# The 128 half rows of w_down: loaded ahead of wq into a buffer of their own

## The chip, the cores and the metric

The kernel runs on one core of one Trainium2 chip. The metric is the device time of one execution in microseconds (us). Before the change it is 202.81 us, the median of three runs (202.72 to 202.81).

The core has the engines TensorE (PE; its weight loads are listed as PEld), VectorE (DVE), ScalarE (ACT), GpSimd (POOL) and SyncE (SP). SP issues nearly all loads here; 16 DMA engines carry them.

## What is computed

One token goes through one decoder layer: attention over a cache of 4,096 positions with 32 heads of 128, then a gated feed-forward part. All tensors are bf16.

```python
x = A_x                                             # 1 x 640
q = layernorm(x) @ wq                               # 640 x 4096, 32 heads of 128
p = softmax(q . k_cache / sqrt(128))                # 32 heads, 4096 positions
h = x + (p . v_cache) @ wo                          # 4096 x 640
g = layernorm(h) @ w_gate                           # 640 x 1728
u = layernorm(h) @ w_up                             # 640 x 1728
out = h + (gelu(g) * u) @ w_down                    # 1728 x 640
```

The tensors that have to be read are large beside the arithmetic: k_cache and v_cache have 33.6 MB each, wq and wo 5.2 MB each, w_gate, w_up and w_down 2.2 MB each.

## The kernel before

**Heads and slots.** The 32 heads are handled in 8 groups of 4. One load brings K or V of one group (4,096 KB, 128 partitions x 32 KB) into one of three slots (`slots`, L114). The order of loads (L191) is K0, V0, K1, V1 and so on to V5, then K6, K7, V6, V7; load n goes to slot n modulo 3, and waits for the last reader of load n - 3 (`issue`, L201 to L209).

**A group's work.** For K: four products of a quarter slot with the query on DVE (L295, `prod`), each summed over part of the head dimension by eight matmuls with the identity on PE (L305 and L29) and by a reduction on DVE (L312). Then the maximum (L317 to L320), the exponential on ACT (L323) and its spreading over four columns on DVE (L326). For V: 32 matmuls (L341 and L29), a masking product and a reduction on DVE (L353 and L363). `matmul_again` (L27, so L29 in the profile) issues a matmul that keeps the weights of the one before.

**The order on each engine.** Each engine has a list of operations, filled by the Python code from top to bottom, and runs it in that order. `P.op` and `P.dma` append to such a list; `_run` (L91) puts a wait ahead of an operation for each event that it depends on. `P.emit({"sync": 2})` (L581) puts the first two operations of SP's list ahead of the barrier that ends the program's preamble; all others stand behind it. As the list of SP stands, these two are the load of wq (L190) and that of K0.

**SP's list.** The load of wq into the arena, the 16 loads of K and V, two loads of wo into the arena (L454 and L455, 2,560 KB each, after the query projection has read wq there), and then the weights of the feed-forward part. These reuse two slots: w_gate and w_up go to the slot that held V6 (`sl[0]`), w_down to the slot that held K7 (`sl[1]`). `free[0]` is the last V6 matmul and `free[1]` the last K7 product (L457).

**w_down.** Its 1,728 rows are split: rows 0 to 1535 as three blocks of 4 x 128 rows (`wd_d`, loaded in four pieces of 640, 640, 480 and 160 KB), rows 1536 to 1663 as one block (column ranges of 64 and 96 KB at the end of the list), and the last 64 rows as 128 half rows of 320 columns (L464; 640 B in each of the 128 partitions, 80 KB), two halves of a row side by side in neighbouring partitions. The half rows went to place 13 of the buffer `wd_sb`, so their load waited for `free[1]`, and it stood first behind wo.

**The last steps.** After the last group, the attention output is multiplied with wo (L399), the residual and the second LayerNorm follow (L480 to L500), then the gate products (L508, `ga`), the up products, gelu on DVE and ACT, and the down products (L558). The down products run block by block: blocks 0 to 3, the half rows (`down([13])`, five matmuls, with the activations doubled and masked in `hm2`), blocks 4 to 7, 8 to 10, 11, and 12 in four column ranges, each followed by a copy to `out_row` (L575 and L577). The output is then stored (L578).

Of the kernel before, what the change touches and what calls it, by code (L numbers as in the profile page):

```python
# [6 lines left out]
BF16 = mybir.dt.bfloat16  # L7
# [4 lines left out]
D = 640  # L12
# [98 lines left out]
def bass_sequential_preLN__gqa_block_cached__glu_gated_geglu__decode_kernel(nc, A_x, A_k_cache, A_v_cache, A_wq, A_wo, B_x, B_w_gate, B_w_up, B_w_down, out):  # L111
    sb = lambda name, shape, dt: nc.alloc_sbuf_tensor(name, shape, dt)
# [41 lines left out]
    sel2 = sb("sel2", [64, 64, 2], BF16)  # L154
    par_t = sb("par_t", [128, 2, 64], BF16)
    par = sb("par", [128, 2], FP32)
    one_bf = sb("one_bf", [1, 1], BF16)
    ones_f = sb("ones_f", [128, 128], FP32)
    mean_f = sb("mean_f", [128, 128], FP32)
# [13 lines left out]
    ps_d = bank[4][:, 264:456]  # L173
# [7 lines left out]
    P = Prog(nc)  # L181
# [5 lines left out]

    A(lambda e: e.preload_act_table_set("natural_log_exp_and_others"))
    d_x = P.dma("scalar", x_row[:, :], A_x[0, :, :])
    d_wq = [P.dma("sync", arena[:, :], A_wq[:, :].rearrange("(p c) n -> p (c n)", c=5))]  # L190
    order = [(kind, G) for G in range(NG - 2) for kind in "KV"] + [(kind, G) for kind in "KV" for G in (NG - 2, NG - 1)]  # L191
    pos = {t: n for n, t in enumerate(order)}
# [251 lines left out]
    for kind, G in order:  # L444
# [3 lines left out]
        if G != NG - 2:  # L448
# [8 lines left out]
    free = [consumed[len(order) - NSLOT + i] for i in (1, 0)]  # L457
    wg_sb = sl[0][:, 0:5 * DF].rearrange("p (c n) -> p c n", c=5)
    wu_sb = sl[0][:, 5 * DF:10 * DF].rearrange("p (c n) -> p c n", c=5)
    wd_sb = sl[1][:, 0:14 * D].rearrange("p (m n) -> p m n", m=14)  # L460
    wu_v = B_w_up[:, :].rearrange("(p c) n -> p c n", c=5)
    wd_v = B_w_down[0:1536, :].rearrange("(a p r) n -> p a r n", a=3, r=4)
    wd_d = wd_sb[:, 0:12, :].rearrange("p (a r) n -> p a r n", a=3)
    d_wd = [P.dma("sync", wd_sb[:, 13, 0:320], B_w_down[1664:1728, :].rearrange("f (s n) -> (f s) n", s=2), free[1])]  # L464
    d_wg = P.dma("sync", wg_sb, B_w_gate[:, :].rearrange("(p c) n -> p c n", c=5), free[0])
    d_wu = [P.dma("sync", wu_sb[:, 0:3, :], wu_v[:, 0:3, :]),
            P.dma("sync", wu_sb[:, 3:5, :], wu_v[:, 3:5, :])]
    d_wd += [P.dma("sync", wd_d[:, a, lo:hi, :], wd_v[:, a, lo:hi, :])
             for a, lo, hi in ((0, 0, 4), (1, 0, 4), (2, 0, 3), (2, 3, 4))]
    d_wl = [P.dma("sync", wd_sb[:, 12, a:b], B_w_down[1536:1664, a:b]) for a, b in (CUT[0:3:2], CUT[2:5:2])]  # L470

# [8 lines left out]
    hi = [V(lambda e: e.tensor_copy(A_hi[0:97, 0:320], bank[0][0:97, 0:320]), pr),  # L480
          A(lambda e: e.copy(A_hi[0:97, 320:640], bank[1][0:97, 0:320]), pr)]
    lo = [V(lambda e, t=t: e.tensor_sub(A_lo[0:97, 320 * t:320 * t + 320], bank[t][0:97, 0:320], A_hi[0:97, 320 * t:320 * t + 320]),
            hi[t]) for t in range(2)]
# [63 lines left out]
    def down(ms, qs=range(4)):  # L547
        def fn(e):
            for m in ms:
                for q in qs:  # L550
                    lo, hi = CUT[q], CUT[q + 1]
                    if m < 13:
                        parts = [(hm[:, m:m + 1], lo, hi, 0)]
                    else:
                        parts = [(hm2[:, s:s + 1], max(lo, 320 * s), min(hi, 320 * s + 320), 320 * s) for s in range(2)]
                    for w, a, b, base in parts:
                        if a < b:
                            i = e.matmul(ps_d[32 * q:32 * q + 1, a - lo:b - lo], w, wd_sb[:, m, a - base:b - base],  # L558
                                         start=False, stop=(m == 12), skip_group_check=(m == 13))
            return i  # L560
        return fn
# [48 lines left out]
```

## Time and profile before

| | |
|---|---|
| median of the runs | 202.81 us |
| the profiled execution's own time | 202.6 us |
| its span, first to last instruction | 201.3 us |
| DVE busy | 136.4 us (68%) |
| PE busy | 114.6 us (57%) |
| bytes read, mean rate | 84.23 MB, 418 GB/s |
| SP's loads (queue q1), share of 16 engines | 97.9% |
| wq, issue to landing | 15.3 us |
| half rows of w_down, issue to landing | 13.7 us |
| mean granted clock of PE | 0.828 |

The profile is of one execution. Its times count from the span's start. An engine is busy while it executes; issuing a load is not counted as busy. A packet of a DMA is here one row of one partition; a packet record has its start, duration and size. Landing is the moment at which the last of the 16 engines reports its share of a load. The granted clock is the part of TensorE's full speed that the throttle allowed; here it changes between 1.0 and 0.5. A wait is put down to what came last. A merged line of the timeline ("x20") covers several instructions.

### The profile page before, as it was taken

How to read it: one execution, taken by the hardware profiler on the slowest of the kernel's cores; microseconds unless marked ns; L12 is line 12 of the kernel's file. 1: busy time of each engine (PE TensorE's matmuls, PEld its weight loads, DVE VectorE, ACT ScalarE, POOL GpSimd, SP SyncE). 2: the span in 40 equal slices, each digit the busy share in tenths (PEclk: the TensorE clock that was granted, in tenths of full speed). 3: DMA queues.
4: the chain of work that ended last, by engine and by line, in shares of the span. 5: the costliest groups of instructions: out<-in, count | busy, mean ns of one | idle time of the engine just before them, and what ended most of it. 6: DMA issues, size and time to landing. Idle time of an engine off the chain costs nothing.

```text
span 201.3 us, 1448 instructions
## 1 busy us (share of the span) xinstructions
PE 114.6 (57%) x785; PEld 17.8 (9%) x381; DVE 136.4 (68%) x168; ACT 8.9 (4%) x27; POOL 4.7 (2%) x14
## 2 busy tenths in 40 slices
PE   0108059537736962777169618762774099386485
PEld 0101000000001000100010001000100001021332
DVE  1300188637995999399757985996799978862531
ACT  2100000000000000000000000000000000000111
POOL 7100000000000000000000000000000000000000
PEclk9999757996995899699757975998899859967575
DMA  9999999999999999999999999999999999999992
GB/s 350 423 392 462 449 417 417 417 443 462 433 430 417 412 423 436 456 449 423 417 417 420 449 449 443 423 417 423 423 462 430 443 423 400 431 415 430 414 407 104
DMA packets 4185, 84.31 MB, mean 419 GB/s; under 512 B 466, under 2 KB 980, under 8 KB 1492
## 3 DMA queue, kind: packets, MB, share of 16 engines
q1 hardware_dynamic: 4178, 84.23, 97.9%
q8 instruction: 4, 0.07, 0.1%
q14 instruction: 1, 0.01, 0.0%
q10 hardware_dynamic: 2, 0.00, 0.0%
HBM read 84.23 MB, written 0.00 MB: 418 GB/s over the span
## 4 chain that ended last, share of the span: by engine, by line
DMA 54%; DVE 28%; PE 15%; SPq 1%; issue 1%; ACT 0%
DMA slot<-in_A_k_cache_dram 41%; DVE prod L295 18%; DMA slot<-in_B_w_down_dram 13%; PE bank L29 10%; DVE sc L312 5%; DVE po_r L363 3%; PE bank L341 2%; PE bank L305 2%; SPq L60 1%; DVE p_bd L326 1%; PE bank L558 1%; DVE mx L317 1%; DVE mxd L319 0%; DVE mxd L318 0%; DVE nb L320 0%
## 5 line engine op out<-in xcount | busy, mean ns | idle before, releaser
L295 DVE TENSOR_TENSOR prod<-slot,qb 128x4096 bf16<-128x4096 bf16 x32 | 72.5, 2286 | 20.8 <-DMA slot<-in_A_k_cache_dram 20.8
L29 PE MATMUL bank<-prod,id_b 128*128 128x512 bf16 x224 | 61.2, 419 | 0.0
L305 PE MATMUL bank<-prod,id_b 128*128 128x512 bf16 x32 | 14.1, 440 | 36.2 <-DVE prod L295 36.1
L341 PE MATMUL bank<-slot,p_bd 128*32 128x512 bf16 x128 | 17.7, 542 | 27.4 <-DVE p_bd L326 27.4
L312 DVE TENSOR_REDUCE sc<-bank 128x32 f32<-128x512 f32 x32 | 22.0, 688 | 9.6 <-PE bank L29 9.5
L29 PE MATMUL bank<-slot,p_bd 128*32 128x512 bf16 x128 | 18.0, 550 | 0.0
L305 PEld LDWEIGHTS bank<-prod,id_b 128*128 128x128 bf16 x32 | 3.3, 102 | 89.8 <-DVE prod L295 89.6
L363 DVE TENSOR_REDUCE po_r<-po_m 128x128 f32<-128x1024 f32 x6 | 11.2, 1865 | 0.0
L353 DVE TENSOR_TENSOR po_m<-bank,m 128x1024 f32<-128x1024 f32 x8 | 9.7, 1218 | 1.6 <-PE bank L29 1.6
L323 ACT ACTIVATE p_t<-sc,nb 128x128 bf16<-128x128 f32 x8 | 3.2, 401 | 150.6 <-DVE nb L320 150.6
L341 PEld LDWEIGHTS bank<-slot,p_bd 128*32 128x32 bf16 x128 | 4.3, 122 | 54.2 <-DVE p_bd L326 40.2
L285 DVE CAST qb<-bank 128x512 bf16<-128x512 f32 x1 | 0.7, 692 | 9.9 <-PE bank L29 9.9
L280 PE MATMUL bank<-arena,xlnB 128*32 128x512 bf16 x20 | 3.3, 627 | 7.1 <-DMA arena<-in_A_wq_dram 7.1
L326 DVE TENSOR_TENSOR p_bd<-p_t,hs 128x512 bf16<-128x512 bf16 x8 | 5.5, 682 | 1.1 <-ACT p_t L323 1.1
L369 PE MATMUL bank<-po_r,hs 128*16 128x129 f32 x16 | 4.3, 367 | 0.8 <-DVE po_r L361 0.8
L399 PE MATMUL bank<-arena,aP 128*1 128x320 bf16 x32 | 4.0, 440 | 0.9 <-DMA arena<-in_A_wo_dram 0.9
L508 PE MATMUL bank<-slot,hlnT 128*1 128x512 bf16 (+1 forms) x40 | 3.5, 450 | 1.5 <-DVE hlnT L497 1.5
L252 PE MATMUL bank<-one_bf,x_row 1*128 1x1 bf16 x5 | 0.4, 177 | 6.9 <-DMA x_row<-in_A_x_dram 6.9
L29 PE MATMUL bank<-arena,aP 128*1 128x320 bf16 x32 | 3.9, 436 | 0.0
L29 PE MATMUL bank<-arena,xlnB 128*32 128x512 bf16 x20 | 3.2, 607 | 0.0
L558 PE MATMUL bank<-slot,hm 128*1 128x128 bf16 (+2 forms) x57 | 2.6, 301 | 0.4 <-DMA slot<-in_B_w_down_dram 0.4
L369 PEld LDWEIGHTS bank<-po_r,hs 128*16 128x16 f32 x16 | 2.0, 130 | 7.4 <-issue 5.8
(89 smaller groups left out, 45.8 us busy)
## 6 DMA issues: line engine op xcount, KB each, us to landing
slot<-in_A_k_cache_dram SPq DMA_DIRECT2D x8, 4096.0 KB, 19.1
slot<-in_A_v_cache_dram SPq DMA_DIRECT2D x8, 4096.0 KB, 18.8
arena<-in_A_wq_dram SPq DMA_DIRECT2D x1, 5120.0 KB, 15.3
arena<-in_A_wo_dram SPq DMA_DIRECT2D x2, 2560.0 KB, 27.6
slot<-in_B_w_gate_dram SPq DMA_DIRECT2D x1, 2160.0 KB, 18.5
slot<-in_B_w_up_dram SPq DMA_DIRECT2D x1, 1296.0 KB, 21.1
slot<-in_B_w_down_dram SPq DMA_DIRECT2D x2, 640.0 KB, 24.4
slot<-in_B_w_up_dram SPq DMA_DIRECT2D x1, 864.0 KB, 22.7
```

Of the source, the lines that this page charges most:

```text
L29: return e.add_instruction(mybir.InstMatmult(name=nc.get_next_instruction_name(), engine=e.engine, start_tensor_calc=start, stop_tensor_ca ...
L295: m = V(lambda e: e.tensor_tensor(out=prod[:, s % 4, :, :], in0=kt[:, 32 * u:32 * u + 32, :], in1=qb[:, G, :].unsqueeze(1).to_broadcast([1 ...
L305: i = e.matmul(*args, start=True, stop=False)
L312: reds[s] = V(lambda e: e.reduce_sum(sc[:, (s // 4) % 2, s % 4, :], ps_f[s % 2][:, :].rearrange("p (g d) -> p g d", d=16), axis=AX.X), fol ...
L326: pbs[G] = V(lambda e: e.tensor_tensor(out=p_bd[:, G % 2, :, :], in0=p_t[:, G % 2, :].unsqueeze(2).to_broadcast([128, 128, 4]), in1=hs[:, ...
L341: return e.matmul(*args, start=(c < 4), stop=(c >= 12))
L353: mks[G] = V(lambda e: e.tensor_tensor(out=po_m[:, :, :], in0=po[:, :].rearrange("p (b d) -> p b d", b=8), in1=m8[:, :].unsqueeze(2).to_br ...
L363: evs[G] = V(lambda e: e.reduce_sum(po_r[:, G % 4, 0:DH], po_m[:, :, :].rearrange("p b d -> p d b"), axis=AX.X), mks[G], hds.get(G - 4))
L369: return e.matmul(ps_a[0:16, 132 * (G // 4):132 * (G // 4) + DH + 1], hs[:, 12 - 4 * g:28 - 4 * g], po_r[:, G % 4, :], start=(g == 0), sto ...
L399: r = e.matmul(*args, start=start, stop=stop)
L508: i = e.matmul(po[32 * a:32 * a + 1, 512 * k:512 * k + n], hlnT[:, c:c + 1], w[:, c, 512 * a:512 * a + n], start=(c == 0), stop=(c == 4))
L558: i = e.matmul(ps_d[32 * q:32 * q + 1, a - lo:b - lo], w, wd_sb[:, m, a - base:b - base], start=False, stop=(m == 12), skip_group_check=(m ...
```

## The change

A buffer `wh_sb` of 128 x 320 elements is added. The half rows are loaded into it by the first load of SP's list, with no wait. The four pieces of the three w_down blocks name `free[1]` as what they wait for, which the half rows' load had waited for ahead of them. The down products with the half rows read `wh_sb`. As the number of operations ahead of the barrier stays 2, the load of K0 is now behind it.

```diff
@@ buffers
+    wh_sb = sb("wh_sb", [128, D // 2], BF16)
@@ start of SP's list
+    d_wh = P.dma("sync", wh_sb[:, :], B_w_down[1664:1728, :].rearrange("f (s n) -> (f s) n", s=2))
     d_wq = [P.dma("sync", arena[:, :], A_wq[:, :].rearrange("(p c) n -> p (c n)", c=5))]
@@ behind wo
-    d_wd = [P.dma("sync", wd_sb[:, 13, 0:320], B_w_down[1664:1728, :].rearrange("f (s n) -> (f s) n", s=2), free[1])]
     d_wg = P.dma("sync", wg_sb, B_w_gate[:, :].rearrange("(p c) n -> p c n", c=5), free[0])
     d_wu = [P.dma("sync", wu_sb[:, 0:3, :], wu_v[:, 0:3, :]),
             P.dma("sync", wu_sb[:, 3:5, :], wu_v[:, 3:5, :])]
-    d_wd += [P.dma("sync", wd_d[:, a, lo:hi, :], wd_v[:, a, lo:hi, :])
+    d_wd = [d_wh] + [P.dma("sync", wd_d[:, a, lo:hi, :], wd_v[:, a, lo:hi, :], free[1])
              for a, lo, hi in ((0, 0, 4), (1, 0, 4), (2, 0, 3), (2, 3, 4))]
@@ down products
-    i = e.matmul(ps_d[...], w, wd_sb[:, m, a - base:b - base],
+    i = e.matmul(ps_d[...], w, (wd_sb[:, m, a:b] if m < 13 else wh_sb[:, a - base:b - base]),
```

More of the change, by code (lines that the diff above doesn't have):

```diff
@@ L557, in fn @@
                         if a < b:
-                            i = e.matmul(ps_d[32 * q:32 * q + 1, a - lo:b - lo], w, wd_sb[:, m, a - base:b - base],
+                            i = e.matmul(ps_d[32 * q:32 * q + 1, a - lo:b - lo], w, (wd_sb[:, m, a:b] if m < 13 else wh_sb[:, a - base:b - base]),
                                          start=False, stop=(m == 12), skip_group_check=(m == 13))
```

## The prediction

> **What bounds the kernel now.** I read the page first (engine shares, the row of 40 slices, the chain that ended last), then the windows at both ends of the span, SP's own timeline, the chain in order of time, and the packet records of the trace.
>
> ```profile
> span 201.3 us, 1448 instructions
> ...
> DMA  9999999999999999999999999999999999999992
> ...
> DMA 54%; DVE 28%; PE 15%; SPq 1%; issue 1%; ACT 0%
> ```
>
> The reader is to see that the 16 DMA engines are busy in every slice but the last. The chain's 28% DVE and 15% PE are steps beside that stream, passed through because a load was issued when a slot came free; they cost nothing while older loads fill the queues. So the time is: start of the stream + packet time of 84.23 MB + what follows the last landing. A change that moves 80 KB within the stream can act only on the start, the end, or the order of landings.
>
> The start, first by windows (columns: stretch, length, the engines' busy us and counts, granted clock, DMA share, GB/s):
>
> ```profile
> 0.00:1.00 1.00, 0.00 (x0) 0.00 (x0) 0.00 (x0) 0.00 (x0) 0.20 (x4) 1.00 0.00 0
> 1.00:2.00 1.00, 0.00 (x0) 0.00 (x0) 0.38 (x5) 0.74 (x1) 0.74 (x1) 1.00 2.18 655
> ```
>
> A packet is counted where it starts. 655 GB/s over 1 us is 16 packets of 40,960 B, one on each engine: the first row of wq. They occupy 2.18 us each on average. The packet records give 1.51 us for the later rows of wq, so each engine first waited some 0.67 us for data, after about 1.0 us in which nothing ran. Then SP:
>
> ```profile
> 0.00 0.39 SPq L60 DMA_DIRECT2D arena<-in_A_wq_dram  x1
> 0.44 0.42 SPq L60 DMA_DIRECT2D slot<-in_A_k_cache_dram  x1
> 1.26 0.33 SPq L60 DMA_DIRECT2D slot<-in_A_v_cache_dram  x1
> ...
> 152.75 0.91 SPq L60 DMA_DIRECT2D arena<-in_A_wo_dram  x2
> 170.10 0.33 SPq L60 DMA_DIRECT2D slot<-in_B_w_down_dram  x1
> 170.48 0.43 SPq L60 DMA_DIRECT2D slot<-in_B_w_gate_dram  x1
> ```
>
> The second load is issued 0.44 us after the first; the third stands behind the barrier that ends the program's preamble (1.26). The load at 170.10 is the one that moves. And the end, by the chain in order of time:
>
> ```profile
> 172.85 25.67 DMA slot<-in_B_w_down_dram
> 198.52 0.04 issue
> 198.56 1.20 PE bank L558 x17
> 199.76 0.03 issue
> 199.79 0.35 DVE out_row L575
> ```
>
> The 480 KB part of w_down (rows 8 to 10 of the third block) lands at 198.52; the last down products, a copy and the output follow.
>
> **The change part by part.** The order of instructions in the changed program has the same instructions on PE, DVE, ACT and POOL; on SP, one load moves from behind wo to the head. Three things follow.
>
> (1) *At its old place it goes.* The packet records show 128 packets of 640 B with 4.10 us in sum: 4.10 / 16 = 0.256 us on each engine, without a gap, plus 0.009 for the completion. Landing bears it out: issue at 170.10 + 13.7 us (its row of DMA issues, 80 KB) = 183.8, against 183.6 for the second half of wo before it (issue at 153.2, 30.4 us, the longest of the arena's loads). Bounds 0.20 and 0.27; I take **-0.26**. Its 0.33 us of issue on SP also go, at no gain: the loads behind it, issued from 170.48 on, land 18 us and more later, so they stand in a queue.
>
> (2) *At the head it comes in.* The load is issued first, wq 0.44 later. Lower end: wq's data flow only the 0.26 us later that the small packets occupy, when wq's descriptors arrive while the small rows still wait for their first data (0.67 of wait is longer than 0.44 of issue). Upper end by issue: wq's first packet starts 0.44 later and waits as long as now, so everything is 0.44 later and the small rows lie inside that. A far end, that the two waits add up, is a rival below (0.67 + 0.26 = 0.93). A gain at the head has no mechanism except that of the fourth case. I take the middle of the two near ends, **+0.35**, as both rest on a row of their own and the wait covers one of them only in part.
>
> In sentences of their own: the Trainium skill ("DMA: Bandwidth & Descriptors", section "Bandwidth", Measured) speaks against such a load: it gives 0.95 us for 64 KB and says that transfers under 64 KB are dominated by descriptors; those are loads from the other kind of queue, GpSimd's. The trace differs where the load lies in a full queue (0.26 us for 80 KB). Where it stands alone at the head no run shows it; with 0.95 there, an estimate from that page, the sum would be +0.69 and the time 203.3 by the profile, 203.5 by the median.
>
> (3) *The order changes.* K0, now third, moves behind the barrier: 0.44 to 1.26. Cover: wq's 5 MB keep the engines until about 15 (landing 15.3), so 13 us are left; without it K0 would be 0.8 late. V0 and K1 slide by one place, under the same cover. The wait for the slot's last reader (K7's product, DVE, 170.1) moves from this load to the first 640 KB of w_down; w_gate and w_up, 4,320 KB, now wait only for the PE's V6 products (about 168.9 in the timeline), and can be issued 1.6 us earlier. Behind the waiting instruction stand only the rest of w_down's loads and the output; nobody waits for their issue, since the queue then holds both halves of wo until 183.6. So no gain and no loss. The buffer of 640 B per partition is new; the down products with the half rows read it in place of the slot, five matmuls as before.
>
> What is before the old place lands 0.35 later, what is behind it 0.35 - 0.26 = **+0.09** later. That matters once: a compute chain starts with wo's second half.
>
> ```profile
> 183.75 0.43 PE L399 MATMUL bank<-arena,aP 128*1 128x320 bf16 x4 [0.91 <-DMA arena<-in_A_wo_dram]
> ...
> 196.77 1.44 PE L558 MATMUL bank<-slot,hm 128*1 128x128 bf16 x37
> ...
> 198.56 1.15 PE L558 MATMUL bank<-slot,hm 128*1 128x128 bf16 x20 [0.35 <-DMA slot<-in_B_w_down_dram]
> ```
>
> PE waits for wo's landing; from there LayerNorm, gate, up and the first 37 down products follow almost without a load ending last, and the last 20 wait 0.35 us for w_down. The chain is put back by 0.26 against the landing that ends its wait: 0.35 - 0.26 = 0.09 us of slack is left. It still does not set the end.
>
> **Sum**: -0.26 + 0.35 = +0.09, say +0.1 us. On the profiled execution (202.6 us, span 201.3 and 1.3 around it) 202.7. That execution lies 0.2 under the median of the three runs (202.81), so for the median: **202.9 us**. What a measurement of this kernel can tell from no change is about 0.2%, 0.4 us.
>
> **The rivals.**
> - *Slower: the head waits twice.* Place: the engines' start. wq's first rows begin their 0.67 us wait only after the small load is through, so the stream starts 0.93 later and gets 0.26 back: +0.67, 203.3 by the profile, **203.5** for the median. For it: the first packets show a wait that no later packet has, and nothing in the trace shows two such starts overlap. Against it: everywhere else packets follow without gap, so the next descriptors are taken while the last are under way. It counts as slower when wq's first data come over 0.67 us later than now (0.67 - 0.26 = 0.41).
> - *Slower: PE becomes the bound.* The 0.09 us of slack is used up if PE is granted less clock after the gate. In the windows 194 to 197 the granted clock is 1.00, and the 20 up matmuls take 1.25 us; at 0.50, the gate's first 17 take 1.87, that is 2.2 for 20. Then +0.95 - 0.09 + 0.09, about **203.8**. Against it: the three runs agree within 0.09 us, so the grant does not fall differently by chance.
> - *A little faster: a late engine catches up.* The first packets of 15 engines end between 3.22 and 3.68 (packet records), of one at 4.39, and this engine's 16th count ends the 480 KB part at 198.52, the next at 198.35. If the small rows take up its late start, up to 0.17 goes on top of the lower end (0.00): **202.6**; with the other engines' spread (198.22) 202.5.
> - *The change doesn't do what it says: the load is hidden anyway.* As the stream is full, to carry 80 KB earlier saves nothing but position; this is the forecast's core, not another time.
>
> **How the numbers follow.** Forecast (0.00 to +0.18, the sums with both near ends): 0.62, all within 0.2%. Head waits twice: 0.20, of which 0.01 stays within 0.2%. PE bound: 0.06, slower. Late engine: 0.12, of which 0.05 for a gain of 0.4 us and more, if the other engines' spread goes too. Faster 0.05, within 0.2% 0.62 + 0.07 + 0.01 = 0.70, slower 0.25. The range reaches from 202.5 (late engine) to 203.5 (head waits twice); the PE case and the rest outside it hold about 0.15. The forecast's own range is 202.8 to 203.0.
>
> **What would show it.** In the changed profile, the windows at the start should have small packets from about 1.0 us and wq's landing (first q matmul at 15.45 now) 0.26 to 0.44 later; by 0.9 and more if the head waits twice. The idle time of DVE ahead of K0's first product should end that much later than 25.03. The DMA row should stay at 9 until the last slice. wo's second half should land as much later as wq; the last large w_down part between 198.5 and 198.7. PE's wait ahead of the last 20 products should shrink from 0.35 to about 0.1. If wq lands late by more than 0.67, step 2 is wrong; if that wait is gone and the end later than w_down's landing asks for, step 3; if the end does not follow w_down's landing, the reading of the bound.

## The result

The changed kernel takes 203.05 us (median of 17 runs, 202.88 to 203.8), the kernel before, beside it, 202.73 (17 runs, 202.59 to 203.06). The ratio is 1.0018, 95% interval 1.001 to 1.0025: 0.18% or about 0.36 us slower (0.32 us by the medians), clear of noise. The bound of 0.2% lies inside the interval. The profiled execution takes 202.89 us against 202.6.

The page of the changed kernel, its row of slices and its chain by engine:

```profile
span 201.6 us, 1448 instructions
...
DMA  8999999999999999999999999999999999999993
...
DMA 53%; DVE 28%; PE 16%; issue 1%; SPq 0%; ACT 0%
```

The reader is to see that the stream still has no gap, and that the two slices which differ are the first (8 for 9) and the last (3 for 2): it starts later and ends later. SP's timeline and the windows of the start, changed kernel:

```profile
0.00 0.40 SPq L60 DMA_DIRECT2D wh_sb<-in_B_w_down_dram  x1
0.46 0.41 SPq L60 DMA_DIRECT2D arena<-in_A_wq_dram  x1
1.28 0.33 SPq L60 DMA_DIRECT2D slot<-in_A_k_cache_dram  x1
```

```profile
0.00:1.00 1.00, 0.00 (x0) 0.00 (x0) 0.00 (x0) 0.00 (x0) 0.20 (x4) 1.00 0.00 0
1.00:1.50 0.50, 0.00 (x0) 0.00 (x0) 0.15 (x2) 0.23 (x1) 0.23 (x1) 1.00 0.63 164
1.50:2.50 1.00, 0.00 (x0) 0.00 (x0) 0.23 (x4) 1.00 (x1) 0.93 (x2) 1.00 2.33 655
```

164 GB/s over 0.5 us is 82 KB: the small packets all start in this half microsecond, and hold the engines for 0.31 us each (0.63 of 0.5). The 16 first packets of wq (655 GB/s over 1 us) start only behind 1.5. Before, 13 of them started in that half microsecond:

```profile
1.00:1.50 0.50, 0.00 (x0) 0.00 (x0) 0.17 (x2) 0.24 (x1) 0.24 (x1) 1.00 3.59 1065
```

The end, by the chain in order of time and by the timeline of the changed kernel:

```profile
171.49 27.31 DMA slot<-in_B_w_down_dram
198.79 0.04 issue
198.84 0.94 PE bank L559 x16
```

```profile
184.25 0.31 PE L401 MATMUL bank<-arena,aP 128*1 128x320 bf16 x4 [1.17 <-DMA arena<-in_A_wo_dram]
...
193.57 2.16 PE L509 MATMUL bank<-slot,hlnT 128*1 128x512 bf16 x20
...
197.31 0.50 PE L559 MATMUL bank<-slot,hm 128*1 128x128 bf16 x16
...
197.68 0.54 PE L559 MATMUL bank<-slot,hm 128*1 128x128 bf16 x16
...
198.84 1.16 PE L559 MATMUL bank<-slot,hm 128*1 128x128 bf16 x20 [0.61 <-DMA slot<-in_B_w_down_dram]
```

The 480 KB part of w_down lands at 198.79, 0.27 after the time before, and the output follows by as much: the execution is 0.29 longer. That part is not the last one waited for. By the trace's records the products behind it wait for each of the three pieces that are left, and the last weight load starts 0.04 us after the landing of the last 96 KB, before (199.35) as after (199.62). The landings between (records of the trace, the middle of the 16 engines' counts, before and after) say where it comes from:

| landing | before | after | later by |
|---|---|---|---|
| wq | 14.31 | 14.93 | 0.62 |
| wo, second half | 182.07 | 182.67 | 0.60 |
| w_gate | 187.40 | 187.80 | 0.40 |
| w_down, 480 KB | 197.05 | 197.44 | 0.39 |

By wq's landing 0.6 us are lost; they stay lost through 168 us of full stream, and 0.2 come back where the half rows used to lie. The last of the 16 counts, for which the products wait, moves by 0.75 at wq (15.31 to 16.06), 0.51 at wo, 0.29 at w_gate and 0.27 at the end; which engine is last is not the same one throughout.

### The profile page after: what moved, and what is told of

Same layout as the page of the kernel before. It is cut to its first block, busy times and chain, and to the rows that moved or that the text cites. A ratio compares the mean times of both kernels' runs of the same rounds, so it can differ in the third digit from the quotient of the medians.

```text
span 201.6 us, 1448 instructions
## 1 busy us (share of the span) xinstructions
PE 113.6 (56%) x785; PEld 17.3 (9%) x381; DVE 136.2 (68%) x168; ACT 8.9 (4%) x27; POOL 4.7 (2%) x14
## 4 chain that ended last, share of the span: by engine, by line
DMA 53%; DVE 28%; PE 16%; issue 1%; SPq 0%; ACT 0%
DMA slot<-in_A_k_cache_dram 39%; DVE prod L297 18%; DMA slot<-in_B_w_down_dram 14%; PE bank L29 11%; DVE sc L314 5%; PE bank L343 3%; DVE po_r L365 3%; PE bank L307 2%; DVE p_bd L328 1%; DVE mx L319 1%; PE bank L559 0%; DVE mxd L321 0%; DVE mxd L320 0%; SPq L60 0%; DVE nb L322 0%
## 5 line engine op out<-in xcount | busy, mean ns | idle before, releaser
L343 PE MATMUL bank<-slot,p_bd 128*32 128x512 bf16 x128 | 18.3, 561 | 27.3 <-DVE p_bd L328 27.3
L29 PE MATMUL bank<-slot,p_bd 128*32 128x512 bf16 x128 | 18.3, 561 | 0.0
L509 PE MATMUL bank<-slot,hlnT 128*1 128x512 bf16 (+1 forms) x40 | 4.5, 544 | 1.5 <-DVE hlnT L498 1.5
L371 PE MATMUL bank<-po_r,hs 128*16 128x129 f32 x16 | 3.8, 328 | 1.5 <-DVE po_r L363 1.5
L401 PE MATMUL bank<-arena,aP 128*1 128x320 bf16 x32 | 2.5, 301 | 1.2 <-DMA arena<-in_A_wo_dram 1.2
L29 PE MATMUL bank<-arena,aP 128*1 128x320 bf16 x32 | 2.6, 317 | 0.0
L319 DVE TENSOR_REDUCE mx<-sc 128x1 f32<-128x128 f32 x8 | 2.3, 286 | 0.3
```

The source lines that it names most:

```text
L29: return e.add_instruction(mybir.InstMatmult(name=nc.get_next_instruction_name(), engine=e.engine, start_tensor_calc=start, stop_tensor_ca ...
L319: m = V(lambda e: e.reduce_max(mx[:, G:G + 1], sc[:, G % 2, :, :].rearrange("p u g -> p (u g)"), axis=AX.X), reds[4 * G + 3])
L343: return e.matmul(*args, start=(c < 4), stop=(c >= 12))
L371: return e.matmul(ps_a[0:16, 132 * (G // 4):132 * (G // 4) + DH + 1], hs[:, 12 - 4 * g:28 - 4 * g], po_r[:, G % 4, :], start=(g == 0), sto ...
L509: i = e.matmul(po[32 * a:32 * a + 1, 512 * k:512 * k + n], hlnT[:, c:c + 1], w[:, c, 512 * a:512 * a + n], start=(c == 0), stop=(c == 4))
```

## The experiments

Two theories of the loss at the head. The *issue theory*: wq starts later by the distance of two issues on SP, whatever the first load carries, as long as that is through in this time. The *sum theory*: the first load's transfer and a new first wait add up. Each ratio is against the kernel before on the same chip.

**The price of the head, by size.** One more load ahead of wq, everything else as before.

```diff
+    ex_sb = sb("ex_sb", [128, 320], BF16)              # 32 elements for 8 KB, 1,920 for 480 KB (there rows 0 to 383)
+    d_ex = P.dma("sync", ex_sb[:, :], B_w_down[1664:1728, :].rearrange("f (s n) -> (f s) n", s=2))
     d_wq = [...]
```

With 8 KB: 

> The kernel before, with one more load ahead of wq: the first 64 B of each of the 128 half rows (8 KB) into a buffer that nobody reads; the half rows stay at their old place. Issue theory: wq starts later by the distance of two issues on SP (0.46 us in the changed kernel's profile), whatever the size of the first load as long as it is through in that time: +0.5 us against before, wq lands about 0.5 later. Sum theory: wq starts later by the transfer of what is ahead of it and then has its first wait anew, about 0.3: with next to no transfer +0.3 us. If the head costs nothing by itself: 0.0.

With 80 KB: 

> The kernel before, with a second copy of the half rows (80 KB) loaded ahead of wq into a buffer that nobody reads. This is the price of the head alone, without the gain at the old place. Issue theory: the same as with 8 KB, +0.5 us. Sum theory: 0.26 more than with 8 KB, +0.55 us. Both: the changed kernel's +0.3 comes back as this price less about 0.23.

With 480 KB: 

> The kernel before, with 480 KB (rows of 3,840 B, 1.22 us on each engine) loaded ahead of wq into a buffer that nobody reads. Issue theory: wq's issue lies inside the transfer, so the price is the transfer alone, +1.2 us. Sum theory: transfer and a new first wait, +1.5 us.

| ahead of wq | median, before | ratio, interval | wq's first packets: mean start, mean time | wq lands (middle count) |
|---|---|---|---|---|
| nothing (before) | | | 1.28, 2.18 | 14.31 |
| 8 KB | 203.13, 202.72 | 1.0024, 1.0016 to 1.0033 | 1.70, 2.29 | 14.94 |
| 80 KB | 203.20, 202.72 | 1.0027, 1.0017 to 1.0038 | 1.66, 2.37 | 14.92 |
| 480 KB | 203.74, 202.72 | 1.0063, 1.004 to 1.0085 | 2.81, 1.56 | 15.28 |

8 KB cost +0.41 us and 80 KB +0.48; a tenth of the bytes has the same price, and wq lands at the same time. The sum theory wanted 0.25 us between them and falls: the intervals of the two times alone would leave room for it, wq's landings, 14.94 and 14.92, do not. 480 KB cost 1.02 by the medians, below the issue theory's 1.2 and far below the sum theory's 1.5. That interval is wide (0.8 to 1.7 us; one of six runs took 205.3), but the trace agrees: wq lands 0.97 later, w_down's 480 KB part 1.05 (198.52 to 199.57). Behind a transfer longer than SP's next issue, wq's first packets take 1.56 us, hardly more than the 1.51 of all later ones, so their wait passes under the transfer. (The 480 KB rows have a wait of their own: 1.52 us on each engine by the records, where eight packets of 0.149 make 1.19.)

One figure shows why the issue counts. Take the mean start of wq's first packets plus what they take beyond 1.51, and count it from wq's issue: 1.95 us before, 2.04 behind 8 KB (wq issued at 0.44), 2.07 behind 80 KB (0.45), 2.06 in the changed kernel (0.46). wq's data flow about 2 us after wq's issue, with or without a small load ahead; only the 480 KB, which keep the engines until 2.8, make it 2.42. So the price of a small load is the distance of the issues and 0.1 us more. Why the data take 2 us no run shows.

**The same load elsewhere.**

```diff
 half_second:     d_wq = [...]
                 +d_wh = P.dma("sync", wh_sb[:, :], ...)          # behind wq, ahead of K0
 half_act:       +d_wh = P.dma("scalar", wh_sb[:, :], ...)        # ACT's first operation
                 -P.emit({"sync": 2})
                 +P.emit({"sync": 2, "scalar": 1})
 half_old_place: +d_wh = P.dma("sync", wh_sb[:, :], ...)          # behind wo, no wait
```

> The changed kernel with its first two loads exchanged: wq, then the half rows, then K0. Both theories of the head: wq is first again, so the load lies in a full stream as it did behind wo; 0.0 us against before, within 0.1, and wq lands at about 15.3 as before. If instead the new buffer or the moved wait cost the 0.3 us, it stays at +0.3.

Measured 202.76 against 202.72, ratio 1.0001 (0.9993 to 1.001). With the same buffer, the same moved wait and K0 still behind the barrier, the loss is gone as soon as wq is first. wq lands at 14.38, the half rows 0.24 behind it.

> The changed kernel with the half rows' load issued from ACT's queue ahead of the barrier, beside SP's issue of wq instead of ahead of it. Issue theory: SP issues wq at 0.0 again; if the small rows pass in the first wait of the engines, -0.2 us against before, if wq's descriptors wait for theirs, between 0.0 and +0.3. Sum theory: small rows ahead of wq cost as at the head, +0.3; behind wq 0.0.

Measured 202.74 against 202.75, ratio 1.0003 (0.9994 to 1.0012): the 0.0 of the list. ACT issues at 0.12, but the first small packet starts at 3.10, behind the first packet of wq on its engine, and by 8 us only 53 of the 128 have started: they go in among wq's packets. The idle time before the first data is not used.

> The changed kernel with the half rows' load back behind wo, still into the buffer of its own and still without a wait: the buffer and the moved wait alone. Both theories of the head: 0.0 us against before, within 0.1. If the buffer or the moved wait cost something, up to +0.3.

Measured 202.93 against 202.75, ratio 1.0009 (1.0000 to 1.0018). This is inconclusive by itself; the run with the load in second place has the same buffer and wait and costs nothing, so I don't put a price on either.

**The gain at the old place, and K0.**

> The changed kernel without the load of the half rows: their buffer is set to zero by POOL, so the last 64 rows of w_down are left out of the result. This is the gain at the old place alone: -0.26 us against before by the packet records (bounds 0.20 and 0.27), under either theory of the head.

Measured 202.47 against 202.75, ratio 0.9992 (0.9983 to 1.0000): -0.28 us by the medians, 0.16 by the ratio, which agrees with 0.26 within its interval. Price of the head with 80 KB and this gain: 0.48 - 0.28 = +0.20 by medians, 0.0027 - 0.0008 = 0.0019 by ratios, against +0.32 and 0.0018 measured for the change. Within their intervals, each some 0.2 us to either side, the two parts make up the whole.

> The changed kernel with three instead of two of SP's operations ahead of the barrier, so that K0 is issued before it again. Both theories of the head: as the changed kernel, +0.3 us against before, since K0 has 13 us of cover. If K0's later issue cost part of it, less than +0.3.

```diff
-    P.emit({"sync": 2})
+    P.emit({"sync": 3})
```

Measured 203.34 against 202.75, ratio 1.003 (1.0018 to 1.0042), whose interval meets that of the change: with K0 issued ahead of the barrier again nothing is won back, so its later issue is no part of the loss. The end of its timeline:

```profile
184.75 0.43 PE L401 MATMUL bank<-arena,aP 128*1 128x320 bf16 x4 [0.27 <-DVE aP L390]
...
194.94 1.25 PE L509 MATMUL bank<-slot,hlnT 128*1 128x512 bf16 x20
...
198.46 1.88 PE L559 MATMUL bank<-slot,hm 128*1 128x128 bf16 x32
199.16 0.28 PEld L559 LDWEIGHTS bank<-slot,hm 128*1 128x1 bf16 x12 [0.20 <-DMA slot<-in_B_w_down_dram]
```

The last 32 down products stand in one row without a wait, as if the compute chain had overtaken the loads. The weight loads show that it has not: the one at 199.16 waits for the 480 KB part, which lands at 199.12, and the last one of all starts 0.04 after the landing of the last 96 KB (199.97). The chain has next to no slack left ahead of the 480 KB part, but the end still follows the landings: this part lands 0.60 later than before, and the execution is 0.64 longer. The next run puts more on the chain.

**Another part at the head.** The 480 KB piece moves, the half rows stay.

```diff
+    w3_sb = sb("w3_sb", [128, 3, D], BF16)
+    d_w3 = P.dma("sync", w3_sb[:, :, :], B_w_down[0:1536, :].rearrange("(a p r) n -> p a r n", a=3, r=4)[:, 2, 0:3, :])
     d_wq = [...]
...
-    d_wd += [P.dma("sync", wd_d[:, a, lo:hi, :], wd_v[:, a, lo:hi, :])
+    d_wd += [d_w3 if (a, lo) == (2, 0) else P.dma("sync", wd_d[:, a, lo:hi, :], wd_v[:, a, lo:hi, :])
```

> The kernel before, with another part of w_down moved to the head: its 480 KB piece (rows 8 to 10 of the third block) into a buffer of its own, the half rows at their old place. Head price +1.0 us (as measured with 480 KB ahead of wq), gain at its old place 1.22 us of packets. If the stream alone sets the end: -0.2 us. If the compute chain from wo's landing becomes the bound, since wo lands 1.0 later and only 0.35 us of slack stands behind it: +0.5 to +0.7 us.

Measured 203.16 against 202.70, ratio 1.002 (1.0008 to 1.0031), from 202.45 to 203.71. The single runs fall apart by PE's mean granted clock: the four at 0.839 and above take 202.45 to 202.72, the six at 0.82 and below 203.10 to 203.71 (correlation -0.91). The two rivals of the expectation are its two ends: with much clock the stream's time comes out (202.45 is 0.25 under 202.70), with little, it seems, the chain's. The profiled execution (202.5, clock 0.839) is of the first kind. Its chain that ended last shows no wait for a load:

```profile
197.97 1.42 PE bank L560 x43
199.39 0.27 DVE out_row L577
```

But here too the trace's records have the last weight load 0.04 us behind the landing of the last 96 KB (199.30), and the granted clock was full from 194.90 to 201.72. None of the longer executions was profiled; that the chain sets the end there is argued from the clock and not shown. The correlation alone would prove little, as the run with wq's first 480 KB split off, below, has -0.74 within 0.19 us; what stands out is the spread of 1.26 us.

**The first wait of wq.** Does it go by the size of the first rows?

```diff
+    wq_f = A_wq[:, :].rearrange("(p c) n -> p (c n)", c=5)
+    d_wq = [P.dma("sync", arena[:, a:b], wq_f[:, a:b]) for a, b in ((0, 1920), (1920, 20480))]    # or 4096
```

> The kernel before, with wq loaded in two pieces, first 3,840 B of each partition (480 KB), then the rest; the half rows at their old place. In the earlier run with 480 KB ahead of wq, the first rows waited some 0.3 us in place of 0.67, and wq's rows behind them hardly. If the engines' first wait goes by the size of the first rows: 0.3 to 0.4 us faster than before, and wq lands that much earlier. If the wait is the same for every first load that is longer than SP's next issue: 0.0.

> The same with a first piece of 8,192 B of each partition (1 MB). If the first wait goes by the size of the first rows: between the split at 480 KB and before, 0.2 to 0.4 us faster. Otherwise 0.0.

> The changed kernel with wq in two pieces (480 KB, rest). The issue distance of 0.46 us at the head stays, the wait of wq's first rows should shrink. Issue theory with a wait by the size of the rows: +0.3 less 0.3, about 0.0 us against before, and 0.3 to 0.4 slower than the split without the half rows at the head. If the whole loss at the head were the first wait of large rows: as fast as the split alone or 0.2 faster.

Measured, in this order: 202.69 (ratio 1.0001, 0.9992 to 1.0009), 202.64 (0.9997, 0.9988 to 1.0006) and 203.18 (1.0026, 1.0016 to 1.0036), before 202.70. My guess on the size of the rows falls: the split brings nothing. The first rows of 3,840 B of wq hold each engine for 1.89 us where eight packets of 0.149 make 1.19, so 0.70 us of wait stay, as with rows of 40,960 B (0.67). With the half rows at the head the loss stays as well, 0.0025 between the third run and the first. What wq waits for in those 0.7 us is left open: the half rows at the head hardly wait (0.31 us by the records against 0.26 in a full queue), w_down's 480 KB 0.33 in one run and 0.57 in the run that moves them, wq 0.57 to 0.86. No version beats the kernel before by more than its interval.

## Why the prediction was right, by its steps

The time lies in the range of 202.5 to 203.5 and within 0.2%, but not in the forecast's own range: +0.09 us was forecast, at most +0.18, and 0.32 to 0.36 came out; 203.05 lies over 202.8 to 203.0. That the change stayed within 0.2% is partly luck, as its interval reaches 0.25%. And as the kernel before took 202.73 beside it and not 202.81, the forecast of 202.9 looks nearer than its sum was.

**The bound** was read rightly: the stream sets the time, and the change acts through start, end and order. 0.62 us lost at the head were still there at wo, 168 us later.

**Step 1, the old place (-0.26)**: right. The distance from wo's to w_gate's landing shrinks by 0.20, and leaving the load out gives -0.28.

**Step 2, the head (+0.35)**: the mechanism of the upper end was right, the size too small. The upper end was 0.44 from the issue alone. wq's first packets start 0.42 later (1.28 to 1.70), and then wait 0.82 instead of 0.67, which makes 0.57 of the 0.62. I had taken the middle, because I gave part of the small packets' time to cover: the small rows were to wait 0.67 us for their first data while wq's issue came in. They hardly wait: they start at 1.03 and are through at 1.53, where wq's first packet starts (1.51), and 8 KB cost what 80 KB do. The value had to be at the upper end or over it, 0.48 by the run with 80 KB alone. With it the sum would have been +0.22 and the time 203.0 for the median, where 203.05 came out.

The sentence from the Trainium skill ("DMA: Bandwidth & Descriptors", section "Bandwidth"), that transfers under 64 KB are descriptor-dominated, was measured on loads from GpSimd. The trace of SP's loads at the head agrees in that bytes hardly count: 8 KB cost 0.41 us, 80 KB 0.48, each in 128 packets; what counts there is the distance of the issues. The 0.95 us of its table for 64 KB doesn't fit: the sum made with it, +0.69, is twice what was measured.

**The slower rival "the head waits twice"**: its mark was met, its sum was not. A landing is the last engine's, and wq's moved by 0.75, the first q product by 0.74 (15.45 to 16.19), both over 0.67; by the prediction's own sign step 2 was wrong. The middle count moved by 0.62 only. Half of the mechanism came true: wq's first packets begin their wait behind the small load, not beside it. The other half did not: the small packets show no 0.67 us of wait to be added, and the sum, +0.67, is twice the result.

**Step 3, the order**: K0's move costs nothing (expected, shown by the run with K0 ahead of the barrier). The slack of the compute chain I put at 0.09; the profiled execution had 0.61. There PE had full clock in wo's products (0.31 us for four where 0.43 to 0.48 stood before) and half clock in the up products, 2.16 us for the 1.25 of before:

```profile
193.95 1.25 PE L508 MATMUL bank<-slot,hlnT 128*1 128x512 bf16 x20
```

The two nearly cancel: from wo's first product to the first down product it is 13.06 us, before 13.02. The first 37 down products then ran at full clock, 0.91 us for 1.44. With wo's products 0.50 later and the 480 KB part 0.27 later that makes the slack: 0.35 - 0.23 - 0.04 + 0.53 = 0.61. I took the chain's length from one execution, as if fixed. I also took the wait ahead of the 480 KB part for all of the slack. The end waits for the last 96 KB: in each of the fourteen profiles the last weight load starts 0.04 us behind that landing.

So the **rival "PE becomes the bound"** is seen in no profile. In the changed kernel its condition was met, half clock in the up products at the price it named (0.91 of 0.95), and the end did not move by it. It is likely, by the clock, in the longer runs with 480 KB moved. Whether it also made the two slowest of the change's 17 runs (203.59 and 203.8, clocks 0.813 and 0.82) is open: others between 0.803 and 0.821 took 202.9 to 203.19, and no profile of the two exists. My argument against it, that three runs agree within 0.09 us, was about a kernel whose chain had at least 0.35 us of slack: it showed that slack, not a steady clock.

**A late engine catches up**: part of it can be seen (0.75 at wq's last count, 0.27 at the end, while the middle moves from 0.62 to 0.39). The end follows the last count, so the profiled execution lost 0.29 and not 0.39. It did not turn the sign. The 0.05 given to a gain of 0.4 us and more had no sum behind it: the rival's own end at 0.3.

## What to carry to other kernels

In a kernel bound by one gapless stream of loads, a load that changes its place returns only its own packet time there; ahead of the first large load it costs the distance of two issues, here 0.4 to 0.5 us for 8 KB as for 80 KB. Let the largest load be issued first and put small ones behind it, where 80 KB took 0.26 here. The slack of the chain on PE was not one number: the same wait was 0.35 us and 0.61 in two profiles and next to nothing in a third. Read it at the lower granted clock, and against the last landing that is waited for, before a change takes 0.3 us of it.

## What I had not expected of the hardware

- Small rows at the head start to move about 1.03 us after the issue and show next to no first wait (29 to 32 ns for most packets of 640 B), while wq's first packets, already issued at 0.46, start at 1.5 to 2.3 and take 1.8 to 3.3 us. So it is not simply the first packet on an idle engine that waits. Nor is it fixed for a load: behind 480 KB wq's first packets wait 0.05. What sets it is not shown.
- A load from ACT's queue issued 0.12 us after wq's did not slip into wq's first wait; its packets took turns with wq's.
- PE's granted clock takes 0.5 or 1.0, in stretches of 3.41 us or multiples (the trace's clock record), and the changes fall at other places of the span in each profile: the last stretch of full clock is 193.58 to 197.00 in the kernel before and 195.46 to 198.87 in the changed one. One program, the moved 480 KB, takes 202.45 to 203.71 us, the more the lower its mean clock. The Trainium skill ("TensorE: Matmul & The Clock Gate", section "Part 1: The HAM clock gate (the "warmup" mystery)") says that the window is 3,413 ns and free-running, not reset when a kernel starts; the trace agrees on the length, and the other places in each profile are what a free-running window would make.
